# A head's product with v spread over five units instead of three, in a fused attention and feed-forward kernel

## The chip, the cores and the metric

The kernel runs on one core of one Trainium2 chip. The metric is device time in microseconds (us) from the first to the last instruction and what lies around it, median of several runs; smaller is better. A core has five instruction queues that run side by side: PE (matrix products, with its weight loads PEld), DVE (vector), ACT (activations), POOL (GpSimd) and SP (here it only issues DMA transfers). Each queue executes its own instructions strictly in order; semaphores tie the queues together.

## The reference

Attention over 2 batches and 8 heads, 768 tokens, head size 64, where a query sees only the keys of its own cluster; then two feed-forward blocks over the 1536 tokens.

```python
q_assign = argmax(q_n . c_n)        # cluster of each query, per head; k_assign likewise
scores = scale * q @ k.T            # (2, 8, 768, 768)
scores = where(q_assign == k_assign, scores, -1e9)
attn = softmax(scores)
x = (attn @ v)                      # gathered to (1536, 512)
h = x @ w_in;  g = (a0+a1*h+a2*h^2+a3*h^3) / (1+|b0||h|+|b1|h^2+1e-6);  x = g @ w_out
h = x @ w2_in; h = h*softmax(h); h = layernorm(h)*g_ln;  out = h @ w2_out
```

All of it is float32; each product is made of rounded high parts and remainders (names ending in h and l, or 1 and 2).

## The kernel before

The attention part is a loop over 96 units: 16 heads (two batches of eight, n = 0 to 15) times 6 tiles of 128 query tokens (t = 0 to 5). One unit (n, t) does this:

- `unit_scores` (PE, lines 384 and 390): four score matmuls into a PSUM tile `s`. The first two read the operands `q1` and `k1`, the other two `q2` and `k2`, which also hold 16 rows of cluster masks. There are two buffers of `s`, so the scores of a unit wait for the exponential of the unit two before it.
- `unit_max` (DVE, line 395): the row maximum (as a minimum of negated scores).
- `unit_exp` (ACT, line 408): the exponential into `p`, with the row sums into `rs`.

Every second unit `turn_p` (DVE, line 425) transposes two units' `p` into the tile `pt` of the head. When all three transposes of a head are done, which is in unit 1 of the next head, its product with v can begin: `pv_step` (PE, line 435), 12 steps of 8 small matmuls into one four-bank PSUM tile `pv` that has a single buffer. `pv_out` (ACT, line 451) copies the product out in two parts, `u` and `w`.

For each pair of heads, `pair_sums` turns the row sums into factors along the tokens: an addition on ACT (line 460), a reciprocal on DVE (line 461), a transpose on PE (line 473), a copy `rt` on ACT (line 475), then on SP a store `rd` to DRAM (line 477) and two broadcast loads `rb` back (line 480). `pair_fin` on POOL adds `u` and `w` (line 487) and multiplies with `rb` into `xf` (line 501).

`prep_head` makes the operands of a head on POOL: three scalings (line 339) and two subtractions (lines 353 and 358) from the loaded tile `dup`; after it SP puts the mask rows in (lines 362 and 363). The operands have two buffers, by the head's parity, so prep of head n+2 cannot begin before the last scores of head n. `load_head` (lines 193 and 194) loads `dup` two heads ahead, into two buffers; `load_v` (line 202) loads v in four transfers, also into two buffers, so v of head n waits until the product of head n-2 is finished.

Besides, the clusters of the heads are found in sets of four to eight operands ahead of their use (lines 259 to 320; one of their operations is the ranking on POOL, line 285), and the weights of the feed-forward part are converted in the background: `w1f` and `raww` on ACT (lines 135 and 138) and DVE (line 142), `w1h` on ACT and `w1l` on POOL (lines 146 and 147).

The code gives the order in which the units and their side work are recorded; a scheduler then orders each queue by times that it simulates. So a line's place in the loop is only a start, and what a queue really does next is read from the order of the built program.

In the loop before, the product of head n-1 stands in units 3, 4 and 5 of head n, four steps in each; the sums of a pair follow in unit 5; the copies `u` and `w` are made in units 0 and 1 of head n+1; `load_v(n)` stands in unit 2.

Of the kernel before, what the change touches and what calls it, by code (L numbers as in the profile page):

```python
# [15 lines left out]
B, H, S, D = 2, 8, 768, 64  # L16
# [14 lines left out]
def fused_kernel(ctx: ExitStack, tc: tile.TileContext, qT, kT, v, cent, w1, w2i, w2o, gln, coef, centT, cst, out):  # L31
# [13 lines left out]
    def psum2(tag, name):  # L45
        return ps[tag].tile([128, 2, 512], F32, name=name, tag=tag, bufs=2)

    def psum4(name):

        return pvp.tile([128, 4, 512], F32, name=name, tag="pv", bufs=1)  # L50
# [124 lines left out]
    def load_pairs(es, parts=1):  # L175
        for pp, i in es:
            b, p = divmod(pp, 4)
            t = asp.tile([128, S], F32, name=f"pr{pp}{i}", tag="pr", bufs=4)
            raw["p", pp, i] = t
        w = S // parts  # L180
        for c in range(parts):
            for pp, i in es:
                b, p = divmod(pp, 4)
                nc.sync.dma_start(
                    out=raw["p", pp, i][:, w * c:w * c + w],
                    in_=(qT, kT)[i][b, 2 * p:2 * p + 2].rearrange("j d t -> (j d) t")[:, w * c:w * c + w])

    def load_head(n):
        b, h = divmod(n, H)
        for i, src in enumerate((qT, kT)):  # L190
            t = qk.tile([128, S], F32, name=f"dup{n}{i}", tag=f"dup{i}", bufs=2)
            if n:
                nc.sync.dma_start(out=t[0:64], in_=src[b, h])
            nc.sync.dma_start(out=t[64:128], in_=src[b, h])
            raw["d", n, i] = t

    def load_v(n):

        b, h = divmod(n, H)
        t = qk.tile([128, S // 32, D], F32, name=f"v{n}", tag="v", bufs=2)  # L200
        for r in range(4):
            nc.sync.dma_start(out=t[32 * r:32 * r + 32], in_=v[b, h])
        vv[n] = t
# [10 lines left out]
    t = psum4("warm")  # L214
# [55 lines left out]
    def by_token(k, t, o):  # L270
        M = 32 * len(sets[k])
        return nc.tensor.transpose(o, E[k][0][0:M, t * 128:(t + 1) * 128], ident[0:M, 0:M])

    def is_max(k, t0, nt, o):
        g = 2 * len(sets[k])
        sv = o.rearrange("p t (g c) -> p t g c", c=C)
        ev = E[k][1][:, t0:t0 + nt].rearrange("p t (g c) -> p t g c", c=C)
        mx = sm.tile([128, nt, g], F32, name=f"mx{k}{t0}", tag=f"mx{nt}{g}", bufs=2)
        nc.vector.tensor_reduce(mx, sv, axis=AX.X, op=ALU.max)
        nc.vector.tensor_tensor(ev, sv, mx[:, :, :, None].to_broadcast([128, nt, g, C]), op=ALU.is_equal)  # L280

    def rank(k, eng):
        g = 2 * len(sets[k]) * NT
        ev = E[k][1].rearrange("p t (g c) -> p (t g) c", c=C)
        eng.tensor_tensor(ev, ev, rev[:, None, :].to_broadcast([128, g, C]), op=ALU.mult)

    def first_max(k):
        g = 2 * len(sets[k]) * NT
        ev = E[k][1].rearrange("p t (g c) -> p (t g) c", c=C)
        mx = sm.tile([128, g], F32, name=f"my{k}", tag=f"my{g}", bufs=1)  # L290
        nc.vector.tensor_reduce(mx, ev, axis=AX.X, op=ALU.max)
        fv = E[k][2].rearrange("p t (g c) -> p (t g) c", c=C)
        nc.vector.tensor_tensor(fv, ev, mx[:, :, None].to_broadcast([128, g, C]), op=ALU.is_equal)
# [134 lines left out]
    def pv_step(n, i):  # L428
        if i == 0:
            pv[n] = psum4(f"pv{n}")  # L430
        for c in range(2):
            j = 2 * i + c
            for r in range(4):
                sl = slice(32 * r, 32 * r + 32)
                last["pv"] = nc.tensor.matmul(  # L435
                    pv[n][64 * c:64 * c + 64, r, 0:192].rearrange("p (t q) -> p t q", t=NT),
                    lhsT=vv[n][sl, j], rhs=PT[n][sl, :, 32 * j:32 * j + 32],
                    start=(i == 0), stop=(i == S // 64 - 1),
                )
# [3 lines left out]
    def pv_out(n, part):  # L443
        key = n // 2
        if key not in U:
            U[key] = fin.tile([128, S], F32, name=f"u{key}", tag="u", bufs=2)
            W[key] = fin.tile([128, S], F32, name=f"w{key}", tag="w", bufs=1)
        mine = slice(0, 64) if n % 2 == 0 else slice(64, 128)
        other = slice(64, 128) if n % 2 == 0 else slice(0, 64)
        o, src = ((U, mine), (W, other))[part]  # L450
        nc.scalar.activation(
            out=o[key][mine].rearrange("p (t r q) -> p r t q", t=NT, r=4),
            in_=pv[n][src, :, 0:192].rearrange("p r (t q) -> p r t q", t=NT), func=AF.Copy)
        if part:
            del pv[n]

    def pair_sums(key):

        r = rs.pop(key)
        nc.scalar.activation(out=r, in_=r, func=AF.Identity, bias=tiny)  # L460
        nc.vector.reciprocal(r, r)
        if key == 7:

            rw = fin.tile([128, S], F32, name="rw", tag="rb", bufs=1)
            nc.vector.tensor_copy(rw.rearrange("p (t j d) -> p j t d", t=NT, j=2), r[:, :, :, None].to_broadcast([128, 2, NT, D]))
            rb = psum2("s", "rbp")
            for t in range(NT):
                nc.tensor.transpose(rb[:, t // 3, t % 3 * 128:t % 3 * 128 + 128], rw[:, t * 128:t * 128 + 128], ident)
            rsd[key] = rb
            return  # L470

        tp = pv[2 * key + 1][:, 0, 256:384]
        nc.tensor.transpose(tp[0:12], r.rearrange("p j t -> p (j t)"), ident)
        rt = sm.tile([12, 128], F32, name=f"rt{key}", tag="rt", bufs=2)
        nc.scalar.activation(out=rt, in_=tp[0:12], func=AF.Copy)
        d = dram.tile([2, S], F32, name=f"rd{key}", tag="rd")
        nc.sync.dma_start(out=d.rearrange("j (t p) -> (j t) p", p=128), in_=rt)
        rb = fin.tile([128, S], F32, name=f"rb{key}", tag="rb", bufs=1)
        for j in range(2):
            nc.sync.dma_start(out=rb[64 * j:64 * j + 64], in_=d[j:j + 1, :].to_broadcast([64, S]))  # L480
        rsd[key] = rb
# [26 lines left out]
    def spread(gen, n, i0, i1, plan=plan):  # L508
        for i in range(n):
            plan[min(96, i0 + (i1 - i0) * i // n)].append(gen)  # L510
# [39 lines left out]
    for i, (x1, x2, er) in enumerate(((q1[0], q2[0], nc.gpsimd), (k1[0], k2[0], nc.vector))):  # L550
        c, x = raw["p", 0, i], raw.pop(("d", 0, i))
# [29 lines left out]
    for a in range(2):  # L581
        c = slice(384 * a, 384 * a + 384)
        nc.scalar.activation(out=q2[0][64:80, c], in_=ts[a][0:16, 0:384], func=AF.Identity, scale=-BIG, bias=big[0:16])
    for a in (1, 0):
        c = slice(384 * a, 384 * a + 384)
        nc.vector.tensor_copy(k2[0][64:80, c], ts[a][32 * jk:32 * jk + 16, 0:384])  # L586
    for a in range(2):
        c = slice(384 * a, 384 * a + 384)
# [4 lines left out]
    def set1_a():  # L593
        mp1[0] = psum4("set1")
        for a in range(2):
            tp = mp1[0][:, a, 0:3 * M].rearrange("p (t m) -> p t m", t=3)
            for t in range(3):
                by_token(1, 3 * a + t, tp[:, t])
            is_max(1, 3 * a, 3, tp)
        rank(1, nc.vector)  # L600
        first_max(1)
# [22 lines left out]
            yield  # L624

    set1_a()
    units = [(n, t) for n in range(B * H) for t in range(NT)]
    NS = S // 64
    for idx, (n, t) in enumerate(units):
        if idx == ACL:  # L630
            asg.close()
            wh["r"] = ctx.enter_context(tc.tile_pool(name="wh2", bufs=4, side="right"))
        for k in range(3, len(sets)):
            if idx == AT[k] - LD:
                load_pairs(sets[k])
        if t == 3 and 0 < n < B * H - 2:
            load_head(n + 2)
        if t == 0:
            if n >= 1 and n + 1 < B * H:
                spread(prep_head(n + 1), 7, idx, idx + 6)  # L640
        if t == 2:
            load_v(n)
        sp = unit_scores(n, t)
        m = unit_max(n, t, sp)
        if t % 2 and idx > 1:
            turn_p(*divmod(idx // 2 - 1, NT // 2))
        if idx == S1B:
            set1_b()

        if n and t >= 3:  # L650
            for i in range(4 * (t - 3), 4 * (t - 2)):
                pv_step(n - 1, i)
            if t == 5 and n % 2 == 0:
                pair_sums(n // 2 - 1)
        unit_exp(n, t, sp, m)
        if n >= 2 and t < 2:
            pv_out(n - 2, t)
            if t == 1 and n % 2:

                fin_ = pair_fin(n // 2 - 1)  # L660
                for i in (1, 5, 6, 7):
                    plan[min(96, idx + i)].append(fin_)
        run_plan(idx)
# [339 lines left out]
```

## Time and profile before

| | |
|---|---|
| runs | 698.61, 699.12, 1168.8 us; median 699.12 |
| profiled execution | 696.75 us, span 694.9 us |
| granted TensorE clock, mean over the span | 0.943 |
| busy over the span | PE 616.4 us (89%), DVE 494.1 (71%), ACT 437.5 (63%), POOL 391.7 (56%) |
| attention part | from the start to about 269 us |
| POOL waiting for `rb` at line 501 | 62.4 us in 7 waits |
| ACT exponential waiting for DVE's maximum | 73.9 us |

The busy time of a queue is not its limit: a queue that waits is idle, and what it waits for is the thing to find. A row of a timeline gives the start, the duration, the queue, the line, the operation and the tiles (out<-in); in square brackets stands the idle time ahead of it and what ended that idle time. Rows of equal operations in a run are merged, with their count.

### The profile page before, as it was taken

How to read it: one execution, taken by the hardware profiler on the slowest of the kernel's cores; microseconds unless marked ns; L12 is line 12 of the kernel's file. 1: busy time of each engine (PE TensorE's matmuls, PEld its weight loads, DVE VectorE, ACT ScalarE, POOL GpSimd, SP SyncE). 2: the span in 40 equal slices, each digit the busy share in tenths (PEclk: the TensorE clock that was granted, in tenths of full speed). 3: DMA queues.
4: the chain of work that ended last, by engine and by line, in shares of the span. 5: the costliest groups of instructions: out<-in, count | busy, mean ns of one | idle time of the engine just before them, and what ended most of it. 6: DMA issues, size and time to landing. Idle time of an engine off the chain costs nothing.

```text
span 694.9 us, 13771 instructions
## 1 busy us (share of the span) xinstructions
PE 616.4 (89%) x5517; PEld 489.4 (70%) x5517; DVE 494.1 (71%) x648; ACT 437.5 (63%) x796; POOL 391.7 (56%) x363
## 2 busy tenths in 40 slices
PE   6578888767687858899999999999998999999998
PEld 3456566556565647678788877788886888888887
DVE  3789879788877882898896588967679464535350
ACT  2464655676566673999987899877677344444341
POOL 7555546483938743999986889987779200000000
PEclk9798889998888988999999999999999999999999
DMA  9965392847557222333300444210100000000001
GB/s 220 269 182 140 90 253 81 223 136 182 139 141 186 66 69 92 122 97 132 135 1 0 153 122 122 90 60 1 31 1 0 1 1 30 17 31 15 31 16 45
DMA packets 22439, 64.71 MB, mean 93 GB/s; under 512 B 4532, under 2 KB 5640, under 8 KB 22376
## 3 DMA queue, kind: packets, MB, share of 16 engines
q1 hardware_dynamic: 21944, 63.67, 32.4%
q8 instruction: 43, 0.70, 0.5%
q10 hardware_dynamic: 432, 0.17, 0.1%
q14 instruction: 20, 0.16, 0.1%
HBM read 59.16 MB, written 3.19 MB: 90 GB/s over the span
## 4 chain that ended last, share of the span: by engine, by line
PE 34%; POOL 12%; ACT 5%; DVE 5%; issue 3%; DMA 2%; POOLq 0%; ACTq 0%; DVEq 0%
PE hh L855 10%; PE o L906 9%; PE y L779 8%; PE h L727 5%; POOL q L743 3%; POOL gl L762 3%; POOL q L742 2%; POOL w1l L147 2%; POOL vl L147 2%; PE lt L888 2%; DMA rawv<-in_w2i 1%; DVE w1w L142 1%; ACT t L740 1%; ACT y L741 1%; DVE h L755 1%
## 5 line engine op out<-in xcount | busy, mean ns | idle before, releaser
L408 ACT ACTIVATE p<-s,m 128x768 f32<-128x768 f32 x96 | 86.2, 899 | 74.2 <-DVE m L395 73.9
L727 PE MATMUL h<-xhl,w1h 128*128 128x512 f32 x384 | 123.0, 397 | 4.4 <-DVE y L756 2.6
L395 DVE TENSOR_REDUCE m<-s 128x1 f32<-128x768 f32 x96 | 89.2, 942 | 37.3 <-PE s L390 37.2
L384 PE MATMUL s<-k,q 128*128 128x384 f32 x192 | 65.5, 427 | 46.7 <-ACT p L408 46.5
L727 PEld LDWEIGHTS h<-xhl,w1h 128*128 128x128 f32 x384 | 72.5, 190 | 22.1 <-DVE y L756 3.9
L435 PE MATMUL pv<-pt,v 32*64 32x192 f32 x3072 | 85.4, 360 | 0.4 <-issue 0.4
L425 DVE STREAM_TRANSPOSE pt<-p 128x1536 f32<-128x1536 f32 x48 | 84.5, 1763 | 0.0
L384 PEld LDWEIGHTS s<-k,q 128*128 128x128 f32 x192 | 34.7, 218 | 67.7 <-ACT p L408 52.9
L779 PE MATMUL y<-gl,w1h 128*128 128x512 f32 x192 | 76.7, 400 | 5.6 <-POOL gl L762 5.6
L435 PEld LDWEIGHTS pv<-pt,v 32*64 32x64 f32 x3072 | 65.5, 148 | 18.0 <-issue 11.1
L779 PE MATMUL y<-gh,w1l 128*128 128x512 f32 x192 | 76.1, 396 | 0.0
L727 PE MATMUL h<-xhl,w1l 128*128 128x512 f32 x192 | 75.9, 395 | 0.0
L762 POOL TENSOR_TENSOR gl<-y,gh 128x512 fp32r<-128x512 f32 x48 | 66.5, 1387 | 10.8 <-ACT gh L761 10.7
L779 PE MATMUL y<-gh,w1h 128*128 128x512 f32 x192 | 69.8, 396 | 0.1
L743 POOL TENSOR_TENSOR q<-q,t 128x512 f32<-128x512 f32 x48 | 65.0, 1354 | 3.1
L390 PE MATMUL s<-k,q 128*128 128x384 f32 x192 | 57.9, 389 | 3.7 <-DVE k L586 2.3
L742 POOL TENSOR_SCALAR q<-t,ab 128x512 f32<-128x512 f32 x48 | 42.2, 879 | 32.2 <-ACT t L740 22.7
L744 DVE TENSOR_TENSOR y<-y,h 128x512 f32<-128x512 f32 x48 | 32.8, 684 | 34.8 <-ACT y L741 34.6
L855 PE MATMUL hh<-vh,xhl 128*128 128x512 f32 x192 | 53.5, 393 | 0.0
L501 POOL TENSOR_TENSOR xf<-u,rb 128x512 f32<-128x512 f32 (+1 forms) x14 | 13.8, 1004 | 62.4 <-DMA rb<-rd 62.4
L779 PEld LDWEIGHTS y<-gl,w1h 128*128 128x128 f32 x192 | 36.5, 190 | 16.9 <-POOL gl L762 9.0
L390 PEld LDWEIGHTS s<-k,q 128*128 128x128 f32 x192 | 41.7, 224 | 4.1 <-issue 2.4
(151 smaller groups left out, 1348.5 us busy)
## 6 DMA issues: line engine op xcount, KB each, us to landing
raww<-in_w SPq DMA_DIRECT2D x32, 512.0 KB, 4.3
v<-in_v SPq DMA_DIRECT2D x64, 192.0 KB, 4.9
dup<-in_qT SPq DMA_DIRECT2D x31, 192.0 KB, 4.2
dup<-in_kT SPq DMA_DIRECT2D x31, 192.0 KB, 5.3
rawv<-in_w2i SPq DMA_DIRECT2D x8, 512.0 KB, 3.6
rawv<-in_w2o SPq DMA_DIRECT2D x8, 512.0 KB, 3.7
out<-ob SPq DMA_DIRECT2D x11, 256.0 KB, 2.0
pr<-in_qT SPq DMA_DIRECT2D x7, 384.0 KB, 4.8
```

The costliest lines, as they stand in the source:

```text
L384: r = nc.tensor.matmul(sp[:, a, 0:384], lhsT=q1[i][:, sl], rhs=k1[i][:, a * 384:(a + 1) * 384], start=True, stop=False)
L390: last["pe"] = nc.tensor.matmul(sp[:, a, 0:384], lhsT=q2[i][:, sl], rhs=k2[i][:, a * 384:(a + 1) * 384], start=False, stop=True)
L395: last["dve"] = nc.vector.tensor_reduce(m, sp[:, :, 0:384], axis=AX.XY, op=ALU.min)
L408: last["act"] = nc.scalar.activation(out=P[n, t // 2][:, t % 2], in_=sp[:, :, 0:384], func=AF.Exp, scale=-1.0, bias=m, accum_out=rs[key][: ...
L425: r = nc.vector.transpose(PT[n][:, 2 * i:2 * i + 2].rearrange("p t k -> p (t k)"), p.rearrange("p t a k -> p (t a k)"))
L435: last["pv"] = nc.tensor.matmul(pv[n][64 * c:64 * c + 64, r, 0:192].rearrange("p (t q) -> p t q", t=NT), lhsT=vv[n][sl, j], rhs=PT[n][sl, ...
L727: r = nc.tensor.matmul(hp, lhsT=w[:, kt * 128:(kt + 1) * 128], rhs=x[:, kt], start=(i == 0), stop=(i == 11))
L743: nc.gpsimd.tensor_tensor(q, q, t, op=ALU.mult)
L762: nc.gpsimd.tensor_tensor(gl, y, gh.bitcast(F32), op=ALU.subtract)
L779: nc.tensor.matmul(o, lhsT=w[:, c], rhs=g, start=(first and i == 0), stop=(last and i == 2))
L855: last["th"] = nc.tensor.matmul(hp[:, a], lhsT=y[:, kt], rhs=w[:, 512 * a:512 * a + 512], start=(kt == 0 and e == 0), stop=(kt == 3 and e ...
L906: r = nc.tensor.matmul(op[:, 0:m], lhsT=l[:, kt], rhs=w, start=(n == 0), stop=(n == 23))
```

## The change

A function `pv_part(n, t)` says which steps of which head's product a unit does. For all but the last head: steps 0 to 1 of head n-1 in unit 3, 2 to 3 in unit 4, 4 to 6 in unit 5; and in the next head, as n-2, steps 7 to 9 in unit 0 and 10 to 11 in unit 1. In head 15 the product of head 14 keeps four steps in each of units 3 to 5, beside the rest of head 13 in units 0 and 1. The pair's sums follow the last step; the copies move from units 0 and 1 to units 1 and 2, the pair's finish from unit 1 to unit 2, and `load_v` from unit 2 to unit 3.

```diff
+    def pv_part(n, t):
+        if t >= 3:
+            c = (0, 4, 8, 12) if n == B * H - 1 else (0, 2, 4, 7)
+            return n - 1, c[t - 3], c[t - 2]
+        return (n - 2, (7, 10)[t], (10, 12)[t]) if t < 2 else (-1, 0, 0)
...
-        if t == 2:
+        if t == 3:
             load_v(n)
...
-        if n and t >= 3:
-            for i in range(4 * (t - 3), 4 * (t - 2)):
-                pv_step(n - 1, i)
-            if t == 5 and n % 2 == 0:
-                pair_sums(n // 2 - 1)
+        m_, i0, i1 = pv_part(n, t)
+        if m_ >= 0:
+            for i in range(i0, i1):
+                pv_step(m_, i)
+            if i1 == NS and m_ % 2 and m_ < B * H - 2:
+                pair_sums(m_ // 2)
         unit_exp(n, t, sp, m)
-        if n >= 2 and t < 2:
-            pv_out(n - 2, t)
-            if t == 1 and n % 2:
+        if n >= 2 and t in (1, 2):
+            pv_out(n - 2, t - 1)
+            if t == 2 and n % 2:
                 fin_ = pair_fin(n // 2 - 1)
```

What this makes of the queues is shown at three places. First PE, from unit 4 of head 10 to unit 2 of head 11, before. `s10_4` is the score tile of unit (10,4), `pv9` the product of head 9, `k10` and `k20` the first and second key operand of even heads, `k11` and `k21` those of odd heads; x16 or x32 counts matmuls.

```order
L384 MATMUL s10_4_2259<-k10_152,q10_150 128x384 x2
L390 MATMUL s10_4_2259<-k20_153,q20_151 128x384 x2
L435 MATMUL pv9_2223<-pt9_2036,v9_2004 64x192 x32
L384 MATMUL s10_5_2304<-k10_152,q10_150 128x384 x2
L390 MATMUL s10_5_2304<-k20_153,q20_151 128x384 x2
L435 MATMUL pv9_2223<-pt9_2036,v9_2004 64x192 x32
L473 MATMUL pv9_2223<-cst_70,rs4_1748 12x128
L384 MATMUL s11_0_2358<-k11_158,q11_156 128x384 x2
L390 MATMUL s11_0_2358<-k21_159,q21_157 128x384 x2
L384 MATMUL s11_1_2374<-k11_158,q11_156 128x384 x2
L390 MATMUL s11_1_2374<-k21_159,q21_157 128x384 x2
L384 MATMUL s11_2_2391<-k11_158,q11_156 128x384 x2
```

The same stretch of PE after:

```order
L384 MATMUL s10_4_2243<-k10_152,q10_150 128x384 x2
L390 MATMUL s10_4_2243<-k20_153,q20_151 128x384 x2
L435 MATMUL pv9_2223<-pt9_2035,v9_2022 64x192 x16
L384 MATMUL s10_5_2272<-k10_152,q10_150 128x384 x2
L390 MATMUL s10_5_2272<-k20_153,q20_151 128x384 x2
L435 MATMUL pv9_2223<-pt9_2035,v9_2022 64x192 x24
L384 MATMUL s11_0_2308<-k11_158,q11_156 128x384 x2
L390 MATMUL s11_0_2308<-k21_159,q21_157 128x384 x2
L435 MATMUL pv9_2223<-pt9_2035,v9_2022 64x192 x24
L384 MATMUL s11_1_2347<-k11_158,q11_156 128x384 x2
L390 MATMUL s11_1_2347<-k21_159,q21_157 128x384 x2
L435 MATMUL pv9_2223<-pt9_2035,v9_2022 64x192 x16
```

The last three fifths of head 9's product now stand behind the scores of (10,5), (11,0) and (11,1), and the transpose of the pair's sums (line 473) goes from ahead of (11,0) to behind (11,1).

Second ACT, from the last exponential of head 8 to that of unit (9,2), before; `rt3`, `u3` and `w3` belong to the pair of heads 6 and 7, `w1f2` and `raww120` to a weight conversion:

```order
L408 ACTIVATE p8_4_1919,rs4_1748<-s8_5_1924,m8_5_1929 128x768
L135 ACTIVATE w1f2_1921<-raww120_1922 128x512
L138 ACTIVATE raww120_1922<-raww120_1922,less_81 128x512
L475 ACTIVATE rt3_1968<-pv7_1835 12x128
L451 ACTIVATE u3_1751<-pv7_1835 64x4x6x32
L451 ACTIVATE w3_1752<-pv7_1835 64x4x6x32
L408 ACTIVATE p9_0_1985,rs4_1748<-s9_0_1978,m9_0_1983 128x768
L408 ACTIVATE p9_0_1985,rs4_1748<-s9_1_1990,m9_1_1995 128x768
L408 ACTIVATE p9_2_2017,rs4_1748<-s9_2_2009,m9_2_2014 128x768
```

The same stretch of ACT after:

```order
L408 ACTIVATE p8_4_1887,rs4_1732<-s8_5_1892,m8_5_1897 128x768
L135 ACTIVATE w1f2_1889<-raww120_1890 128x512
L138 ACTIVATE raww120_1890<-raww120_1890,less_81 128x512
L408 ACTIVATE p9_0_1959,rs4_1732<-s9_0_1928,m9_0_1933 128x768
L408 ACTIVATE p9_0_1959,rs4_1732<-s9_1_1963,m9_1_1968 128x768
L475 ACTIVATE rt3_1992<-pv7_1835 12x128
L451 ACTIVATE u3_1762<-pv7_1835 64x4x6x32
L451 ACTIVATE w3_1763<-pv7_1835 64x4x6x32
L408 ACTIVATE p9_2_2011,rs4_1732<-s9_2_2003,m9_2_2008 128x768
```

The copy of the sums and the two copies of head 7's product move from ahead of the first exponential of head 9 to behind its second one.

Third POOL, from the end of prep of head 10 to the beginning of prep of head 11, before; `e4` is the ranking of the last set of clusters, `xf0` and `xf1` the pair's finish, which waits for `rb3`:

```order
L353 TENSOR_TENSOR k20_153<-dup101_1814,k10_152 64x768
L358 TENSOR_TENSOR q10_150<-dup100_1811,q10_150 64x768
L487 TENSOR_TENSOR u3_1751<-u3_1751,w3_1752 128x768
L501 TENSOR_TENSOR xf0_162<-u3_1751,rb3_1972 128x512
L501 TENSOR_TENSOR xf1_163<-u3_1751,rb3_1972 128x256
L285 TENSOR_TENSOR e4_1805<-e4_1805,cst_70 128x768
L339 TENSOR_SCALAR k11_158<-dup111_2025,sgn_85 128x768
```

The same stretch of POOL after:

```order
L353 TENSOR_TENSOR k20_153<-dup101_1809,k10_152 64x768
L358 TENSOR_TENSOR q10_150<-dup100_1806,q10_150 64x768
L487 TENSOR_TENSOR u3_1762<-u3_1762,w3_1763 128x768
L285 TENSOR_TENSOR e4_1798<-e4_1798,cst_70 128x768
L501 TENSOR_TENSOR xf0_162<-u3_1762,rb3_1996 128x512
L501 TENSOR_TENSOR xf1_163<-u3_1762,rb3_1996 128x256
L339 TENSOR_SCALAR k11_158<-dup111_2019,sgn_85 128x768
```

The ranking now stands ahead of the finish; otherwise POOL's order there is the same. On SP the transfers around a pair's sums, here those of heads 4 and 5, stand after the change as follows:

```order
L193 DMA dup100_1806<-in_qT 64x768
L194 DMA dup100_1806<-in_qT 64x768
L194 DMA dup101_1809<-in_kT 64x768
L202 DMA v7_1604<-in_v 32x1536 x2
L477 DMA rd2_1577<-rt2_1575 12x128
L202 DMA v7_1604<-in_v 32x1536 x2
L480 DMA rb2_1579<-rd2_1577 64x768 x2
```

They stood in this order before it too: the loads for head 10 (`dup100`, `dup101`), two transfers of v of head 7, the store, two more of v, the loads back.

## Rows read from the trace of the kernel before

**Rows 1.** Stretches: length, then busy time of the engines (instructions), PEclk, DMA share, GB/s
```profile
39.01:58.74 19.73, 16.52 (x373) 12.66 (x369) 17.06 (x17) 11.06 (x23) 8.72 (x13) 0.91 0.62 174
77.27:90.19 12.92, 11.56 (x195) 8.41 (x195) 8.07 (x7) 5.61 (x12) 7.82 (x18) 0.74 0.35 97
90.97:211.94 120.97, 93.32 (x1848) 71.65 (x1846) 102.26 (x98) 75.37 (x146) 71.63 (x55) 0.89 0.61 161
211.94:242.40 30.46, 22.91 (x441) 17.82 (x435) 23.70 (x22) 20.20 (x40) 25.70 (x21) 0.83 0.52 130
39.01:269.20 230.19, 177.40 (x3550) 136.31 (x3546) 182.90 (x171) 138.90 (x269) 134.86 (x122) 0.87 0.53 139
```

**Rows 2.** Timeline of PE, units (6,5) to (7,2): start, length, engine, line, operation
```profile
119.92 0.62 PE L384 MATMUL s<-k,q 128*128 128x384 f32 x2
...
120.82 1.56 PE L435 MATMUL pv<-pt,v 32*64 32x192 f32 x64
...
122.33 0.60 PE L384 MATMUL s<-k,q 128*128 128x384 f32 x2
...
127.92 1.01 PE L384 MATMUL s<-k,q 128*128 128x384 f32 x2 [3.94 <-ACT p L408]
```

**Rows 3.** Timeline of ACT, the copies at the end of head 6
```profile
124.95 0.25 ACT L475 ACTIVATE rt<-pv 12x128 f32<-12x128 f32 x1
125.23 0.81 ACT L451 ACTIVATE u<-pv 64x768 f32<-64x768 f32 x1
126.05 0.80 ACT L451 ACTIVATE w<-pv 64x768 f32<-64x768 f32 x1
```

**Rows 4.** Timeline of POOL, attention part
```profile
59.45 0.91 POOL L339 TENSOR_SCALAR k<-dup,sgn 128x768 fp32r<-128x768 f32 x1 [3.48 <-PE s L384]
...
90.97 0.91 POOL L339 TENSOR_SCALAR k<-dup,sgn 128x768 fp32r<-128x768 f32 x1 [5.41 <-issue]
...
120.71 0.91 POOL L339 TENSOR_SCALAR k<-dup,sgn 128x768 fp32r<-128x768 f32 x1 [0.77 <-POOL q L358]
...
140.84 1.95 POOL L501 TENSOR_TENSOR xf<-u,rb 128x512 f32<-128x512 f32 x2 [11.97 <-DMA rb<-rd]
...
150.72 0.91 POOL L339 TENSOR_SCALAR k<-dup,sgn 128x768 fp32r<-128x768 f32 x1 [1.25 <-issue]
...
172.73 1.83 POOL L285 TENSOR_TENSOR e<-e,cst 128x768 f32<-128x768 f32 x1
...
179.41 2.53 POOL L358 TENSOR_TENSOR q<-dup,q 64x768 fp32r<-64x768 f32 x1
182.04 0.91 POOL L339 TENSOR_SCALAR k<-dup,sgn 128x768 fp32r<-128x768 f32 x1
...
208.97 1.82 POOL L358 TENSOR_TENSOR q<-dup,q 64x768 fp32r<-64x768 f32 x1
210.87 3.76 POOL L147 TENSOR_TENSOR w1l<-w1f,w1h 128x512 fp32r<-128x512 f32 x3
```

**Rows 5.** Timeline of SP's transfers: stores of four pairs' sums, one read-back
```profile
99.76 0.34 SPq L477 DMA_DIRECT2D rd<-rt  x1
...
130.77 0.30 SPq L477 DMA_DIRECT2D rd<-rt  x1
...
135.65 1.87 SPq L480 DMA_DIRECT2D rb<-rd  x2
...
160.15 0.30 SPq L477 DMA_DIRECT2D rd<-rt  x1
...
191.65 0.34 SPq L477 DMA_DIRECT2D rd<-rt  x1
```

**Rows 6.** Groups of DVE, heads 5 to 12: shapes, count, busy, mean ns, idle before
```profile
L395 DVE TENSOR_REDUCE m<-s 128x1 f32<-128x768 f32 x49 | 45.4, 939 | 15.8 <-PE s L390 15.6
L425 DVE STREAM_TRANSPOSE pt<-p 128x1536 f32<-128x1536 f32 x25 | 44.1, 1762 | 0.0
```

**Rows 7.** Timeline of PE, second scores of unit (4,0)
```profile
77.27 0.58 PE L390 MATMUL s<-k,q 128*128 128x384 f32 x2 [1.43 <-DMA k<-oh]
```

## What the change should do to the time

> Units are written (n, t): head n of 16, row tile t of 6. "Prep n" is POOL's work that makes the operands of head n. Times are microseconds (us) of the profiled execution.
>
> **What bounds the kernel now.** I read first the busy time by stretch [rows 1]. The change touches only the attention part, from the first product with v at unit (1,3) (39.0) to the start of the feed-forward part (269.2), a third of the span. There no engine is full: PE 177, DVE 183, ACT 139, POOL 135 of 230 us. Eight heads, from (4,5) to (13,0), take 120.97 us, 15.1 each; DVE, the busiest, has 102.26 in them, 12.8 per head. So something is waiting, and the timelines by engine tell what.
>
> PE's timeline [rows 2] shows an uneven head. A unit's scores take 0.90 us (119.92 to 120.82), its share of the product with v, 32 matmuls, 1.51 (120.82 to 122.33). Units 3, 4 and 5 carry all 96, so PE runs through them without idling, 2.4 each, while DVE waits for scores. Then units 0 and 1 have scores alone, and before unit 2 PE idles 3.94 us. ACT's timeline says why [rows 3]: at the head's end it does weight conversions and then the two copies u and w of the finished product, 0.8 each, ahead of the first exponential of the new head, which frees the score buffer that unit 2 needs. Next to the idle time the granted clock is at its lower level: the first scores after it take 1.01 for two matmuls where 0.62 is usual [rows 2].
>
> This is what the change evens out. But POOL's timeline [rows 4] shows a second ring, which doesn't contain the product with v. Take the turn that starts with prep 8 at 120.71. SP can issue the loads for head 10 only as prep 8 frees their buffer; behind them stand two v loads, and behind these the store rd of the row sums, at 130.77 [rows 5]: 10.06 after prep 8 began. The row sums' copy rt had been ready since 125.20 [rows 3], so SP's order, not the sums, fixed that. The read-back rb is issued at 135.65, after rd has landed (4.88); POOL, which stands at xf waiting for rb for 11.97, goes on at 140.84 (5.19 later). Xf and prep 9 take until 149.47 (8.63). Sum: 10.06 + 4.88 + 5.19 + 8.63 = 28.76 for two heads. Only then is POOL free for prep 10, and it waits for PE merely 1.25 before 150.72. The other turns read alike: idle 0.77 ahead of prep 8, 0.10 ahead of prep 12 (prep 11 ends at 181.94), where a turn held the ranking op of 1.83 between xf and prep 11; nothing ahead of prep 14, where three w1l subtractions of 3.76 fill the gap [rows 4]. From prep 6 to prep 14 this ring of POOL, SP and two DMA trips is nearly as slow as PE. That is the limit I expect the change to run into.
>
> **The change, part by part.** (a) The products' count stays; 96 matmuls at 1.51 per 32 are 4.5 us per head, now as 16, 16, 24, 24, 16: 0.75 or 1.13 per unit, so a unit needs PE for 1.65 to 2.05 instead of 0.9 or 2.4. Work added: none.
>
> (b) U and w stand in ACT's order behind the second exponential of the head, no longer ahead of the first. Unit 2's scores then wait for neither. The exponential of unit 2 does, but while ACT spends 1.6 on them, DVE has the 1.76 transpose [rows 6] ahead of that unit's maximum: covered. Without that cover it would cost 1.6 less the overlap per head.
>
> (c) What is late next is DVE: six maxima of 0.94, three transposes of 1.76 [rows 6], and its other work: 12.8 per head on average. With a PE unit below 2.05 and DVE's average unit at 12.8/6 = 2.13, free running would be 2.1 to 2.2 per unit.
>
> (d) Row sums, their copy, rd and rb depend on units one head later: ready after the exponential of (odd head,1), not at the end of the even head. Counted from scores (even,5): 0.90 + 1.13 + 0.90 + 1.13 + 0.90 is 5.0 to the scores of (odd,1), then maximum 0.94, exponential 0.90, rt 0.25: 7.1; with PE at the lower clock, up to 9. SP reaches rd's place 8.8 to 10.1 after the even prep starts (99.76, 130.77, 160.15 and 191.65 [rows 5] against 90.97, 120.71, 150.72 and 182.04 [rows 4]). So rd isn't moved: cost 0, bound 0 to 1 per turn. The v load moved behind the head loads in the code keeps its place in SP's order; the v loads beside rd wait for the product's end at about 5, also before SP gets there. Cost 0, bound 1 per turn.
>
> (e) The ranking op of heads 9 to 11 now stands ahead of xf, inside POOL's wait for rb: that turn falls from 31.2 to 29.4.
>
> The sum goes along the path. (1,3) to (2,5): 8 units in 19.73 [rows 1], now at 2.2 each, 17.6, with set operations on DVE: −2.1, of which I take 1.9. From (2,5) to the second scores of (4,0): 0, since these wait for the mask row's DMA (1.43 idle, [rows 7]), queued behind rb of the same ring. (4,0) to (4,5): 12.92 [rows 1]; 5 units at 2.1 are 10.5: −2.4. POOL can take this 4.3, as it idles 3.48 ahead of prep 4 and 5.41 ahead of prep 6 [rows 4]. From prep 6 to prep 14 only POOL's idle time and the hidden ranking op can go: 0.77 + 1.25 + 0.10 + 1.83: −3.95. (13,0) used to start 1.15 after prep 13's end (210.79); it starts with it: −1.15. (13,0) to (15,0): 30.46; two heads at 12.8 with a restart of 1.2 at the lower clock (three pairs of score matmuls at 0.4 more) are 26.8; POOL's and SP's path is rt at 7.3 after (13,0), the trips 10.07, xf 1.95, one w1l 1.3 and prep 6.7, 27.3, the longer: −3.1. Head 15 carries 40 matmuls of head 13 besides its 96 of head 14, 1.9 us, partly in the old gap: +0.8. Contention on POOL: the last prep op took 2.53 at 179.41 and 1.82 at 208.97 [rows 4]; I allow such delays 0.8 in all: +0.8. Sum: −1.9 − 2.4 − 3.95 − 1.15 − 3.1 + 0.8 + 0.8 = −10.9. The feed-forward part starts earlier and is unchanged.
>
> The Trainium skill (SBUF — State Buffer, Who interferes with whom) says that VectorE instructions with two SBUF inputs lock GpSimd's reads out for their whole length. The 2.53 row lies beside such a VectorE operation (line 310) and agrees; with a delay of 0.7 in each of six turns, 4.2 instead of 0.8, the sum would be −7.5.
>
> The profiled execution took 696.75, 1.85 above its span; the median of the runs is 699.12. The saving is taken off the median: 699.1 − 10.9 = 688.2.
>
> **The rivals.** (1) *The ring gives way.* If rd and rb come back sooner, DVE sets the pace. For: one turn, prep 4 to prep 6, idles long. Against: four turns in a row with 8.8 to 10.1 to rd. Then the eight heads take 102.26 plus about 4 of gaps, 106, not 121: −15 instead of −5; with the other terms −20, 679.
> The Trainium skill (DMA: Bandwidth & Descriptors, Anatomy of one DMA) gives a fixed cost of about 2.0 us per transfer on another queue path. By it both trips would be about 5 instead of 10.07, and this rival would hold; the trace's 4.88 and 5.19 differ, and the sum goes by them.
>
> (2) *Slower: rd becomes late.* The product's last matmuls now stand on PE behind the scores of (odd,0), which wait for the odd prep. If rt comes after SP's slot, every us goes into the ring once per turn, six turns. Point of decision: rt later than 9 to 10 after the even prep starts; my 7.1 to 9 is close. A slip of 2 costs 12, more than all that is won: 700; slower by over 2% needs a slip of 4 or more: 712.
>
> (3) *Little arrives.* Masks and loads pace heads 1 to 4, and SP's and ACT's other work heads 13 and 14, so those terms are lost; the ring gives its 3.95 and no more: 695.2. For: the mask wait [rows 7]; against: POOL's idle time of 3.48 and 5.41 shows that PE was late there.
>
> **How the numbers follow.** Forecast 0.60 (688.2, own range 684.5 to 693); rival 1: 0.14; rival 2: 0.08, rival 3: 0.18. Leaving out the far end of rival 1 and most of rival 2 gives 680.5 to 697. About 2%, 14 us, is what a measurement of this kernel can tell from no change. Faster by more (below 685.1): rival 1 and the low edge of the forecast, 0.20. Slower by more: the far part of rival 2, 0.03. Within: 0.77.
>
> **What would show it.** Right: PE's long idle at unit 2 by ACT is gone, and in its place stands idle time at the scores of odd heads 7, 9, 11, 13, released by POOL's last prep op; POOL's waits for rb stay near 12 us and prep 6 to prep 12 at 29 us per turn; DVE's share of the eight heads rises from 85% to about 89%. Wrong: idle of POOL ahead of even preps (then PE or DVE is slower than I think); rd issued later than 10 after the even prep (rival 2); turns of 26 or less (rival 1).

## The result, and the profile after

| | before | after |
|---|---|---|
| median of the runs | 698.94 us (4 runs, 698.61 to 1168.8) | 690.18 us (4 runs, 689.42 to 690.42) |
| ratio, 95% interval | | 0.9854, 0.9814 to 0.9895 |
| profiled execution, span | 696.75, 694.9 | 690.06, 688.3 |
| busy over the span | PE 616.4, DVE 494.1, ACT 437.5, POOL 391.7 | PE 617.2, DVE 495.3, ACT 438.0, POOL 392.5 |
| granted clock | 0.943 | 0.955 |

The medians lie 8.8 us apart, 1.3%; 688.2 was predicted. The ratio is taken over the fast runs, without the one of 1168.8 us; the quotient of the two medians, 0.9875, lies inside its interval. The two traces show 6.7 us of the difference, since the execution profiled before lay 2.2 under the median of its runs. The steps below are compared trace with trace, so they add up to 6.6 of span. They come from one execution of each kernel, and of 58 executions of before that were measured beside the experiments 57 lay between 695.1 and 705.2 us, so that 1 us in a single step proves little by itself.

First PE after the change, around the start of head 7 (columns as in [rows 2]):

```profile
118.57 1.01 PE L384 MATMUL s<-k,q 128*128 128x384 f32 x2 [2.44 <-POOL q L358]
119.37 0.84 PE L390 MATMUL s<-k,q 128*128 128x384 f32 x2
...
122.16 0.62 PE L384 MATMUL s<-k,q 128*128 128x384 f32 x2
...
125.19 0.62 PE L384 MATMUL s<-k,q 128*128 128x384 f32 x2 [0.34 <-ACT p L408]
```

The idle 3.94 before unit 2 of [rows 2], released by the exponential, is down to 0.34. In its place PE stands idle 2.44 before the head's first scores, and POOL's last preparation op releases it; the scores behind it run at the lower clock, 1.2 GHz (granted 0.50 from 118.57 to 120.40, 1.01 for two matmuls; 0.62 at 122.16, at 2.4). Over the attention part, PE's waits (total, times, longest):

```profile
PE s L384 <- ACT p L408: 13.1, 21, 1.6
PE s L384 <- POOL q L358: 11.7, 4, 3.5
```

Before, the first of these was 41.4 in 19 and the second didn't exist. Now POOL after the change, which answers to [rows 4]:

```profile
88.24 0.91 POOL L339 TENSOR_SCALAR k<-dup,sgn 128x768 fp32r<-128x768 f32 x1 [3.62 <-issue]
...
116.06 2.46 POOL L358 TENSOR_TENSOR q<-dup,q 64x768 fp32r<-64x768 f32 x1
118.61 0.91 POOL L339 TENSOR_SCALAR k<-dup,sgn 128x768 fp32r<-128x768 f32 x1
...
139.27 2.01 POOL L501 TENSOR_TENSOR xf<-u,rb 128x512 f32<-128x512 f32 x2 [10.35 <-DMA rb<-rd]
...
147.62 0.91 POOL L339 TENSOR_SCALAR k<-dup,sgn 128x768 fp32r<-128x768 f32 x1
...
157.26 2.20 POOL L285 TENSOR_TENSOR e<-e,cst 128x768 f32<-128x768 f32 x1 [0.90 <-DVE e L310]
168.83 2.41 POOL L501 TENSOR_TENSOR xf<-u,rb 128x512 f32<-128x512 f32 x2 [9.37 <-DMA rb<-rd]
...
178.25 0.91 POOL L339 TENSOR_SCALAR k<-dup,sgn 128x768 fp32r<-128x768 f32 x1
...
211.79 0.91 POOL L339 TENSOR_SCALAR k<-dup,sgn 128x768 fp32r<-128x768 f32 x1
```

Preps 8, 10 and 12 (118.61, 147.62, 178.25) begin with no idle time, and the ranking at 157.26 lies inside the wait for `rb`. And yet prep 6 to prep 14 takes 123.55 (88.24 to 211.79); it took 123.64 before. What POOL won was lost on SP, as the stores after the change show (answering to [rows 5]):

```profile
99.90 0.34 SPq L477 DMA_DIRECT2D rd<-rt  x1
...
128.99 0.30 SPq L477 DMA_DIRECT2D rd<-rt  x1
...
134.71 1.26 SPq L480 DMA_DIRECT2D rb<-rd  x2
...
158.16 0.30 SPq L477 DMA_DIRECT2D rd<-rt  x1
...
189.44 0.66 SPq L477 DMA_DIRECT2D rd<-rt  x1
```

The four turns of the ring, prep 6 to prep 14, cut at the same four points in both traces:

| piece of the ring, sum of four turns | before | after | difference |
|---|---|---|---|
| even prep starts, to `rd` issued | 37.89 | 43.77 | +5.88 |
| `rd` issued, to `rb` issued | 20.88 | 18.41 | -2.47 |
| `rb` issued, to `xf` | 20.10 | 19.97 | -0.13 |
| `xf`, odd prep, to the next even prep | 44.77 | 41.40 | -3.37 |
| sum | 123.64 | 123.55 | -0.09 |

The windows after the change, cut at the scores of the same units as in [rows 1] (the third from prep 6 to the scores of (13,0)):

```profile
40.02:57.44 17.42, 14.56 (x309) 10.14 (x305) 15.90 (x17) 10.73 (x22) 8.03 (x6) 1.00 0.68 189
76.29:87.45 11.16, 11.10 (x210) 7.42 (x210) 7.93 (x7) 6.06 (x12) 7.97 (x12) 0.85 0.25 71
88.24:208.06 119.82, 92.83 (x1831) 64.37 (x1829) 104.92 (x98) 76.52 (x149) 71.34 (x54) 0.94 0.64 165
208.06:235.80 27.74, 23.75 (x434) 16.43 (x434) 21.51 (x21) 19.11 (x38) 24.79 (x20) 0.89 0.59 150
```

The two short ones and the last lost 2.31, 1.76 and 2.72. The long one, half of the attention part, lost 1.15.

### The profile page after: what moved, and what is told of

Same layout as the page of the kernel before. It is cut to its first block, busy times and chain, and to the rows that moved or that the text cites. A ratio compares the mean times of both kernels' runs of the same rounds, so it can differ in the third digit from the quotient of the medians.

```text
span 688.3 us, 13785 instructions
## 1 busy us (share of the span) xinstructions
PE 617.2 (90%) x5517; PEld 478.0 (69%) x5517; DVE 495.3 (72%) x648; ACT 438.0 (64%) x796; POOL 392.5 (57%) x363
## 4 chain that ended last, share of the span: by engine, by line
PE 35%; POOL 11%; ACT 6%; DVE 5%; issue 3%; DMA 1%; ACTq 0%; POOLq 0%; DVEq 0%
PE hh L864 10%; PE o L915 10%; PE y L788 8%; PE h L736 6%; POOL q L752 3%; POOL gl L771 3%; POOL q L751 2%; POOL vl L147 2%; PE lt L897 2%; ACT h L760 1%; DVE w1w L142 1%; DMA raww<-in_w 1%; ACT t L749 1%; DVE h L764 1%; POOL w1l L147 1%
## 5 line engine op out<-in xcount | busy, mean ns | idle before, releaser
L435 PE MATMUL pv<-pt,v 32*64 32x192 f32 x3072 | 89.1, 352 | 11.0 <-ACT w L451 6.1
L384 PE MATMUL s<-k,q 128*128 128x384 f32 x192 | 64.3, 419 | 31.8 <-ACT p L408 18.8
L425 DVE STREAM_TRANSPOSE pt<-p 128x1536 f32<-128x1536 f32 x48 | 84.5, 1762 | 0.0
L435 PEld LDWEIGHTS pv<-pt,v 32*64 32x64 f32 x3072 | 60.0, 140 | 33.7 <-issue 16.7
L384 PEld LDWEIGHTS s<-k,q 128*128 128x128 f32 x192 | 31.9, 207 | 59.7 <-ACT p L408 27.5
L771 POOL TENSOR_TENSOR gl<-y,gh 128x512 fp32r<-128x512 f32 x48 | 66.7, 1391 | 10.9 <-ACT gh L770 10.8
L751 POOL TENSOR_SCALAR q<-t,ab 128x512 f32<-128x512 f32 x48 | 42.0, 875 | 30.4 <-ACT t L749 20.8
L390 PE MATMUL s<-k,q 128*128 128x384 f32 x192 | 54.2, 367 | 4.5 <-DVE k L586 2.3
L390 PEld LDWEIGHTS s<-k,q 128*128 128x128 f32 x192 | 39.0, 210 | 4.9 <-DMA q<-oh 2.5
```

Of the source, the lines that this page charges most:

```text
L384: r = nc.tensor.matmul(sp[:, a, 0:384], lhsT=q1[i][:, sl], rhs=k1[i][:, a * 384:(a + 1) * 384], start=True, stop=False)
L390: last["pe"] = nc.tensor.matmul(sp[:, a, 0:384], lhsT=q2[i][:, sl], rhs=k2[i][:, a * 384:(a + 1) * 384], start=False, stop=True)
L425: r = nc.vector.transpose(PT[n][:, 2 * i:2 * i + 2].rearrange("p t k -> p (t k)"), p.rearrange("p t a k -> p (t a k)"))
L435: last["pv"] = nc.tensor.matmul(pv[n][64 * c:64 * c + 64, r, 0:192].rearrange("p (t q) -> p t q", t=NT), lhsT=vv[n][sl, j], rhs=PT[n][sl, ...
L771: nc.gpsimd.tensor_tensor(gl, y, gh.bitcast(F32), op=ALU.subtract)
```

## The experiments

The theory: after the change the ring (even prep, dup and v loads, store `rd`, read-back `rb`, `xf`, odd prep) sets the pace of the middle heads. The rivals: DVE sets it, or PE with ACT. The table gives, for each run, the time of eight heads (from the maximum of unit (4,5) to that of (13,0)), the busy time in it, the granted clock there, and the ratio on record to the runs of before on the same chip. That ratio isn't the quotient of the two medians, which lies up to 0.004 from it, each inside the interval. The medians come from several chips, so the ratios are compared; the eight heads are read from one execution of each kernel. Line numbers of the experiments are up to 3 higher than before's.

| kernel | eight heads | PE busy | DVE busy | clock | ratio (95%) |
|---|---|---|---|---|---|
| before | 121.90 | 94.25 | 103.40 | 0.89 | 1 |
| after | 121.27 | 94.28 | 104.92 | 0.93 | 0.9854 (0.9814 to 0.9895) |
| e1 after, `xf` behind the odd prep | 109.99 | 88.55 | 105.06 | 1.00 | 0.9663 (0.9617 to 0.9709) |
| e2 before, `xf` behind the odd prep | 122.11 | 96.72 | 102.29 | 0.86 | 0.995 (0.9919 to 0.9981) |
| e3 after, POOL's odd prep 1.8 longer | 128.52 | 96.88 | 106.26 | 0.92 | 1.0037 (1.0008 to 1.0065) |
| e4 before, copies recorded later | 123.10 | 93.87 | 103.85 | 0.89 | 0.9981 (0.9949 to 1.0014) |
| e5 after, store first on SP | 112.72 | 91.62 | 105.96 | 0.97 | 0.9683 (0.9636 to 0.973) |
| e6 e2 and e4 together | 120.57 | 95.46 | 102.21 | 0.87 | 0.9945 (0.9907 to 0.9983) |
| e7 after, e1 and e5 together | 110.84 | 90.25 | 104.88 | 0.98 | 0.9627 (0.9576 to 0.9678) |
| e8 e2, copies behind the second exponential | 115.93 | 91.33 | 104.78 | 0.93 | 0.9808 (0.9744 to 0.9872) |
| e9 before, copies behind the second exponential | 120.26 | 96.35 | 105.25 | 0.89 | 0.9944 (0.9911 to 0.9977) |
| e10 after, v loads behind the store | 113.97 | 94.78 | 104.65 | 0.96 | 0.9725 (0.9647 to 0.9804) |

### Does the ring hold the kernel after the change?

**e1.** The finish of a pair is put behind the odd head's preparation, so that POOL works while the sums travel (`r` is the `xf` op, `prep` the last op of a preparation).

```diff
+            if key < 6:
+                behind(r, last["prep"])
...
-                for i in (1, 5, 6, 7):
+                for i in (1, 10, 11, 12):
```

> The kernel after, with POOL's finish of a pair (xf, which waits for the read-back rb) put behind the preparation of the odd head instead of ahead of it; nothing else is changed. Ring theory (POOL, SP's queue and two DMA trips set the pace of heads 5 to 13, 30 to 31 us per two heads): POOL prepares the odd head while the sums travel, the ring falls apart, heads run at the pace of DVE, 12.8 to 13.5 each, eight heads take 104 to 110 us instead of 121: 674 to 681 us, 9 to 16 below the kernel after. Rival (DVE, or PE and ACT together, already set the pace after the change and POOL's wait for rb only fills slack): 688 to 692, no change. A third way, POOL prepares the odd head earlier but prep of the next even head then waits for PE, which gains only what POOL idled at rb less what it idles there: 682 to 686.

678.77 us. The eight heads take 11.3 less, and DVE is busy for 95.5% of them. Groups of that stretch (busy, mean, idle before and its releaser), the maximum first after the change and then in e1, where `xf` follows:

```profile
L395 DVE TENSOR_REDUCE m<-s 128x1 f32<-128x768 f32 x49 | 45.2, 935 | 10.7 <-PE s L390 10.3
...
L395 DVE TENSOR_REDUCE m<-s 128x1 f32<-128x768 f32 x50 | 45.8, 930 | 2.4 <-PE s L390 2.1
L501 POOL TENSOR_TENSOR xf<-u,rb 128x512 f32<-128x512 f32 (+1 forms) x8 | 8.4, 1069 | 0.6 <-DMA rb<-rd 0.4
```

The idle time ahead of the maximum falls from 10.7 to 2.4, and POOL's wait for `rb`, 38.6 in the four turns after the change, to 0.6. So DVE was not what held the kernel after the change; in e1 it is busy nearly all the time.

**e3.** The reverse: two more scalings of 0.91 in each odd preparation.

```diff
-        rnd(er, k1[i], c, sgn[:, 1:2])
+        for _ in range(3 if n % 2 and n > 1 else 1):
+            rnd(er, k1[i], c, sgn[:, 1:2])
```

> The kernel after with the first scaling of each odd head's preparation from head 3 on done three times instead of once on POOL: 2 times 0.91 us more of POOL per pair of heads, same result. Ring theory: every turn of the ring grows by 1.8 us, five to six turns, 9 to 11 us more in all, 699 to 701. Rival (POOL has slack, DVE or PE sets the pace): 690 to 692.

703.02 us, 1.0037 against 0.9854: 12.8 us more than after. The eight heads grow by 7.25 and hold four odd preparations, 1.81 each: every microsecond put into the ring comes out at its end. The expectation's 9 to 11 counted five to six turns; the odd heads from 3 to 15 are seven, 12.7. Of PE's waits in that stretch two groups now name POOL, 13.1 together, where it was 11.7 after the change (the exponential stands beside them with 10.6):

```profile
PE s L385 <- POOL k L339: 8.7, 3, 3.0
PE s L391 <- POOL k L354: 4.4, 3, 2.0
```

**e5.** The ring opened at another place: SP issues the store ahead of the loads that stood before it (`r` is each dup load of an even head, `x` each v load of an odd one).

```diff
+                if n % 2 == 0 and "rd" in last:
+                    behind(r, last["rd"])
...
+            if n % 2 and "rd" in last:
+                behind(x, last["rd"])
```

> The kernel after, with the store rd of a pair's sums ahead of the loads for the even head two on (dup) and of the odd head's v in SP's queue; POOL's order is that of the kernel after. If SP's order fixed the store's time, as the prediction read it, rd goes out as soon as rt is there, 5 to 7 us after the even preparation starts instead of 10.4 to 11.7; the turns fall from 30.9 by 4 to 6 until DVE sets the pace (13.75 per head in the kernel after with the finish behind the odd preparation, so 27.5 per turn): 677 to 682. Rival (the sums are late after the change, or the trip through DRAM grows by what the store gains because the same transfers are under way): 687 to 691.

677.63 us. Its POOL timeline has the sign that the prediction gave for a ring that isn't the limit, idle time ahead of an even prep:

```profile
114.86 0.91 POOL L342 TENSOR_SCALAR k<-dup,sgn 128x768 fp32r<-128x768 f32 x1 [4.71 <-issue]
```

Three edits at three places, two that shorten or open the ring and one that lengthens it, move the time the way the ring theory says, and the one that lengthens it by as much as it adds. That the ring sets the pace after the change is shown.

### What was the limit before?

**e2.** The edit of e1 on the kernel before.

> The kernel before with the same edit (xf behind the preparation of the odd head). If before the change the path through PE and ACT (product in three units, copies ahead of the first exponential) was a limit of its own just behind the ring, as the prediction read it (idle of 3.9 us at unit 2 of each head), the gain is small: 2 to 6 us, 693 to 697. If the ring alone set the pace before, and the idle at unit 2 was slack, the gain is as large as with the change: 10 to 16 us, 683 to 689. The difference between this run and the kernel after with the same edit is what the change is worth without the ring: by the prediction's terms 15 to 20 us.

698.01 us, 1 us above the 693 to 697 of the first expectation; by the ratio, 0.995, it is the small gain that this expectation named (3.5 us). The eight heads stay at 122.11. With POOL out of the way (it waits 43.1 for PE ahead of the preparations) PE holds the kernel at the same length. Group of the first scores in that stretch:

```profile
L384 PE MATMUL s<-k,q 128*128 128x384 f32 x100 | 33.9, 425 | 21.6 <-ACT p L408 21.4
```

Two limits of nearly one length stood behind one another: PE with ACT at 122 (here), and the ring at 120 to 121 (e9 below, and the kernel after the change). The change takes away the first; without the second it would have been worth 2.9% (0.995 to 0.9663; 19.2 us between the medians, both from one chip), and with it 1.5%.

### Which part of the change does it?

**e4 and e6.** Of the change, only the place in the code of the copies `u` and `w` and of the pair's finish, one unit later, on before (e4) and on e2 (e6).

```diff
-        if n >= 2 and t < 2:
-            pv_out(n - 2, t)
+        if n >= 2 and t in (1, 2):
+            pv_out(n - 2, t - 1)
```

> The kernel before with one part of the change alone: the copies u and w and the pair's finish move from units 0 and 1 to units 1 and 2; the product stays in three units. If the gain of the change came from the copies standing ahead of the first exponential (idle of 3.9 us before unit 2), most of it comes with this: 690 to 693. If it came from the spreading of the matmuls, 697 to 700, and with rd not moved in SP's order the turns stay at 30 to 32 us. Ring theory adds: whatever PE gains here, prep 6 to prep 14 stays within 2 us of the 123.6 of before.

> The kernel before with the finish xf behind the odd preparation and, of the change, only the copies u and w and the finish one unit later; the product stays in three units. It splits the gain of about 19 us that the whole change has where the ring is out of the way (698.0 against 678.8). If the copies ahead of the first exponential were what held PE at unit 2: 683 to 688, most of it comes. If the three full units of 2.4 us and the two empty ones are what holds, whatever ACT does: 695 to 698. Both halves needed: 689 to 693.

0.9981 and 0.9945, the same as without the edit. But they don't answer the question. In ACT's order the copies still stand ahead of a head's first exponential, as the scheduler put them back there (the product in three units is ready by then); in e6 `w` runs at 141.71 and the exponential of (8,0) behind it at 142.54, and the other heads read alike. What was meant to be moved had not moved.

**e8 and e9.** The copies (`r`) are tied behind the head's second exponential (`after`), on e2 (e8) and on before (e9).

```diff
+        if after is not None:
+            behind(r, after)
...
-        if n >= 2 and t < 2:
-            pv_out(n - 2, t)
+        if n >= 2 and t == 1:
+            pv_out(n - 2, 0, last["act"])
+            pv_out(n - 2, 1, last["act"])
```

> The kernel before with the finish xf behind the odd preparation, and the copies u and w forced behind the second exponential of the head in ACT's order, as they stand after the change; the product stays in three units. (In the runs with the copies recorded one unit later ACT still did many of them ahead of the first exponential, so they didn't take this step apart.) If the copies ahead of the first exponential held PE at unit 2, as the prediction's step (b) has it: 3 to 4 us per head less one maximum, 680 to 688. If three units of 2.4 and two of 0.9 hold the head at 14.5 to 15 us whatever ACT does: 693 to 697, and the idle time before unit 2 stays, released by the exponential, some 2 us long.

> The kernel before with the copies forced behind the second exponential of the head and nothing else: the ring stays closed. Ring theory: whatever it gains in PE's order, the turns from prep 6 to prep 14 stay at 29 to 32 us and the time within 5 us of before: 694 to 699. If the copies are the gain and the ring isn't the limit: 685 to 691, as with the whole change.

With the ring open the copies' place alone brings the eight heads from 122.11 to 115.93, and the rest of the change, the spreading above all, brings 109.99 (e1): 6.2 and 5.9, half each. With the ring closed the same edit leaves 120.26 and 0.9944, so that of the 1.5% which the change is worth as it stands the copies alone bring 0.6. The medians, 684.27 and 695.3, lie where the step (b) and the ring theory put them. (The stretch is the better measure of the halves: the code up to unit (1,3) is the same, but this unit is reached at 43.80 in e8, at 40.71 in e2 and at 39.84 in e1.)

### Why did the ring not shorten?

The store's data are there in time: `rt` ends 6.7 us after prep 8 started (125.04 + 0.25, against 118.61; 5.1 to 7.5 in the four turns), and `rd` is issued 10.38 after it:

```profile
125.04 0.25 ACT L475 ACTIVATE rt<-pv 12x128 f32<-12x128 f32 x1
```

Ahead of it SP's v loads wait, for transfers that are still under way. Waits of the v loads from 88 on, first before, then after:

```profile
SPq L202 <- DMA raww<-in_w: 2.5, 3, 1.2
...
SPq L202 <- DMA v<-in_v: 1.1, 2, 0.6
...
SPq L202 <- DMA pr<-in_kT: 0.3, 1, 0.3
```

```profile
SPq L202 <- DMA raww<-in_w: 4.2, 3, 2.1
...
SPq L202 <- DMA pr<-in_kT: 2.8, 2, 1.5
...
SPq L202 <- DMA v<-in_v: 1.4, 3, 0.6
```

Together 3.9 before and 8.4 after. Not all of them stand ahead of a store; in the four stretches from an even prep to its `rd` they are 2.8 before and 8.1 after. SP's order gives the place: between the last dup load and `rd` only two v loads are issued, and these four gaps grew from 7.65 to 12.44 in sum, 4.79 of the slip of 5.88.

The slip comes even where the sums aren't one unit later. In e9, where product and sums stand as before, `rt` ends 2.5 to 3.9 after the even prep starts, and yet `rd` is issued 9.9 to 11.1 after it, 42.1 in sum of four turns (37.9 before, 43.8 after). One of the turns, prep 8 and its store:

```profile
124.65 0.91 POOL L339 TENSOR_SCALAR k<-dup,sgn 128x768 fp32r<-128x768 f32 x1
...
135.44 0.30 SPq L479 DMA_DIRECT2D rd<-rt  x1
```

A reading that fits both is that where POOL doesn't pause ahead of the even prep, SP's transfers for the two preps follow each other without a pause as well. It isn't shown, and not the whole of it: ahead of prep 12 POOL paused for just 0.10 before the change, and there `rd` slipped by 1.58.

**e10.** Of e5 only the v loads are put behind the store; the dup loads stay ahead of it.

> The kernel after with only the odd head's v loads behind the store rd in SP's queue; the loads dup of the even head stay ahead of it. It splits the gain of the run with the store first (677.6). If the two v transfers ahead of the store are what put it from about 9.5 to 10.9 after the even preparation, and if the store's trip of 2.9 to 5.7 is the wait behind the v and dup loads in the same queue: rd 7.3 to 8.5 after the even preparation, turns 27.5 to 28.5, 679 to 684. If the dup loads matter alone (the store lands behind them whatever stands between): rd 2 us sooner but its trip 2 us longer, 687 to 691.

679.49 us. The store goes out 7.85, 9.60, 8.10 and 9.16 after the even prep (two of them later than expected), 34.7 in sum where it was 43.8. The turns take 27.4, 28.1, 28.0 and, beyond what was expected, 32.0. SP around one store, in e10 and then in e5:

```profile
148.65 1.18 SPq L193 DMA_DIRECT2D dup<-in_kT  x2
149.92 1.19 SPq L193 DMA_DIRECT2D dup<-in_qT  x2
151.49 0.31 SPq L478 DMA_DIRECT2D rd<-rt  x1
153.23 1.00 SPq L201 DMA_DIRECT2D v<-in_v  x2
157.39 1.10 SPq L481 DMA_DIRECT2D rb<-rd  x2
```

```profile
148.66 0.31 SPq L480 DMA_DIRECT2D rd<-rt  x1
149.06 0.79 SPq L203 DMA_DIRECT2D v<-in_v  x2
150.49 1.12 SPq L483 DMA_DIRECT2D rb<-rd  x2
```

Behind four dup loads the store's trip, to the issue of `rb`, is 5.90 (3.2 to 6.0 over the turns), without them 1.83 (1.3 in the other turns, where `rb` is issued as soon as SP has got to it). Taking away the v loads alone didn't shorten it (2.9 to 5.7 after the change). So the trip of 4.88 that the prediction took from [rows 5] as a price was, for the most part, the work of the dup loads issued ahead of the store; whether it waits its turn behind them or shares the way with them isn't shown. The Trainium skill (DMA: Bandwidth & Descriptors, Anatomy of one DMA) gives about 2.0 us as the fixed cost of a transfer on another path; the 1.3 of e5 lies under it, and no run here shows what is in it. Why the issue of a v load waits for the landing of a transfer that has nothing to do with it isn't settled by these runs.

### A version that beats both

**e7.** Both edits on the kernel after.

> The kernel after with both edits: the store rd first in SP's queue and the finish xf behind the odd preparation. If the ring is gone with either of them and DVE sets the pace (busy 94% of heads 5 to 13 with the finish moved alone), the second edit brings nothing: 677 to 680. If the read-back still cost something with the finish moved alone (POOL idled 4.0 us for it in all), up to 4 us: 674 to 677.

673.77 us, just below the second case of the expectation; ratio 0.9627: 26 us below before and 16 below after by the ratios, the lowest median of these kernels. It isn't shown to beat e1: the intervals of the two (up to 0.9678, from 0.9617) overlap, in the eight heads they are alike (110.84, 109.99), and 2.6 of the 5.8 us between their spans lie in the feed-forward part, which neither edit touches.

## Why the prediction was right, and where not

688.2 was the sum, 690.2 the runs' median, 8.8 us below before where 10.9 was forecast. Step by step, from score to score in the two traces:

| step | predicted | measured |
|---|---|---|
| start to (1,3) | 0 | +1.01 |
| (1,3) to (2,5) | -1.9 | -2.31 |
| (2,5) to the second scores of (4,0) | 0 | +0.32 |
| (4,0) to (4,5) | -2.4 | -1.76 |
| ring up to the end of prep 13 | -3.95 + 0.8 | -0.04 |
| (13,0) starts with prep 13's end | -1.15 | -1.10 |
| (13,0) to (15,0) | -3.1 | -2.72 |
| head 15 | +0.8 | +0.45 |
| feed-forward part | 0 | -0.45 |
| sum | -10.9 | -6.6 |

**The bound was read right.** The prediction's second ring, which doesn't contain the product with v, is what kept 122 us at 121; e1, e3 and e5 show it from three sides. The waiting moved where the prediction put it: PE's idle time to the odd heads behind POOL's last op, none ahead of preps 8 to 14. DVE's share of the long stretch rose from 84.5% to 87.6% (89% forecast). Two signs were off: POOL's waits for `rb`, forecast near 12, were 8.9 to 10.4 (it now also stands 0.7 to 3.0 ahead of `u`, for the copy `w`), and the turns from prep 6 to prep 12, forecast at 29, took 30.4, 29.0 and 30.6.

**Steps (a) and (b) were right, and of one size.** The copies' place and the rest of the change bring 6 us each in the eight heads (e8, e1), but only once the ring is open. The prediction's rival 1, 679 if the ring gives way, is near what e5 measured, 677.6, but its terms don't all hold: it has 106 for the eight heads, which took 112.72, and its own terms add up to 678 (-10.9 + 5 - 15).

**Step (d) failed.** "Rd isn't moved: cost 0, bound 0 to 1 per turn" took SP's slot as a fixed time after the even prep, 8.8 to 10.1, and asked only whether `rt` would be late for it. `Rt` was not, as worked out (6.7 against an estimate of 7.1). The slot moved: to 10.4 to 11.7, 1.5 per turn, the sign that the text had named for rival 2, through another mechanism. Some of it came back in the store's trip (-0.6 per turn), and the rest ate the 3.4 that POOL gained. The idle time that (e) and the ring's term had counted as a gain, 0.77 + 1.25 + 0.10 + 1.83, went from POOL, but SP's way from one read-back to the next store took 76.0 in three turns, where it had taken 76.6. That SP fixed the time of `rd` was said in the prediction; that it would then fix the turn as well was not drawn from it. Why the v loads on that way wait longer stays open.

**Contention on POOL** stayed within what was allowed: POOL's piece of the ring lost 3.37, 0.6 less than 3.95, and 0.8 was allowed. Single delays did come, 2.46 at 116.06 for an op of 1.82 (beside VectorE's line 310 at 115.91) and 2.41 at 168.83 for an `xf` of 1.95 (beside its line 142 at 169.79). The Trainium skill (SBUF — State Buffer, Who interferes with whom) says that a VectorE instruction with two SBUF inputs contends with a GpSimd instruction that reads SBUF; these rows agree. But the kernel before had such delays too, and the sum of -7.5 that six more of 0.7 would have given is not what the piece shows.

**The median.** 4.3 us of the sum's 10.9 did not come in the traces, 3.1 of them in the ring and 1.0 in the set-up ahead of (1,3), which the change doesn't touch. That the forecast is only 2 off is owed in part to the 2.2 by which the profiled execution of before lay under its median, and that is luck.

## What to carry to other kernels

Where two limits of one length stand behind each other, a change that takes away one is worth the gap to the other: look for the ring that the edited work isn't in, and open it with one edit before the change is judged. Follow such a ring through the queue that issues the transfers too: an idle engine in it may be covering for that queue, and a small store that others wait for belongs ahead of the large loads. When a step of a change is tried alone, read the queue's order first, since a scheduler may put the work back.

## What the runs showed of the hardware

- A store of 6 KB: 1.3 us, once 1.8, from its issue to the issue of the load that reads it back where no dup loads stood just ahead of it in its queue (e5), 2.9 to 6.0 behind them (after, e10).
- A transfer's issue on SP waited for the landing of earlier transfers to other tiles: 8.1 us for the v loads in the four stretches from an even prep to its store after the change, 2.8 before.
- TensorE's granted clock was lower where PE's stalls were longer: with the same matmuls in the eight heads PE was busy 88.55 at a granted clock of 1.00 with a longest wait for the exponential of 1.9 (e1), and 96.72 at 0.86 with one of 4.0 (e2). A stall of 2.44 ahead of the scores was followed by two at 1.01 instead of 0.62 (after, at 118.57), so a wait on PE can cost more than its length; behind one of 2.19 (after, at 76.29) two still took 0.59, and only the next scores, at 78.30, took 1.01.
